# Second batch's k and q turned on TensorE instead of by the DMA crossbar, in a fused attention and FFN kernel

## The chip, the cores and the metric

The kernel runs on 1 core of one Trainium2 chip. The metric is the device time of one execution in microseconds (us), median of several runs. A run is called fast or slow; on one core a slow run is one that lies over 1.5% above the fastest of the same kernel. Profiles are of single executions; their span is about 2 us shorter than the time quoted for the same run.

Names used below: TensorE is the matmul engine (PE in the profile), VectorE is DVE, ScalarE is ACT, GpSimd is POOL, and the sync queue (SP) issues DMAs. "Turning" means transposing. SBUF and PSUM are the two on-chip memories that hold the tiles of the kernel; its matmuls write to PSUM. A "crossbar turn" is a transpose that the DMA engines do, from SBUF to SBUF. A "TensorE turn" is a matmul with an identity, followed by a copy from PSUM to SBUF on VectorE.

## The reference

Eight batches, eight heads, 576 positions, head dimension 64, feature dimension 128. All inputs and the output are float32.

```python
def phi(x):                                   # per batch and head
    proj = einsum('bhsd,df->bhsf', x, w_phi)
    proj = proj - max(abs(proj), axis=-1)
    return concatenate([exp(proj), exp(-proj)], axis=-1)
q_p, k_p = phi(q), phi(k)
kv  = einsum('bhsf,bhsd->bhfd', k_p, v)
z   = sum(k_p, axis=2)
x   = einsum('bhsf,bhfd->bhsd', q_p, kv) / (einsum('bhsf,bhf->bhs', q_p, z) + 1e-6)
x   = x.transpose(0, 2, 1, 3).reshape(4608, 512)
out = (maximum(x @ w_gate, 0) * (x @ w_val)) @ w_out      # d_ff = 1536
```

## The kernel before

The kernel lists closures at "ticks", sorts them, and emits them in that order; every engine then runs its own instructions in the emitted order. The FFN of batch g runs while the attention of batch g+1 is computed, so that TensorE always has matmuls. Batches are numbered from 0; "the second batch" is b = 1. Of the 576 positions of a batch, 512 go in four chunks of 128; the last 64 of two batches together make one shared ("mixed") chunk.

The projections need k and q with the head dimension on the partitions, so each must be turned after its load. Batch 0 is turned on TensorE, because nothing else is there to do; all later batches go through the crossbar.

```python
def turn(b, name):                                    # the crossbar
    n = H * C // 2
    t = inputs[f"{name}T", b] = sb_in.tile([P, n, P], BF16, name=f"{name}T{b % 2}")
    nc.sync.dma_start_transpose(out=t, in_=inputs[name, b].rearrange("p h c d -> p (h c d)"))

def transposed(blocks):                               # TensorE, then a VectorE copy
    n = len(blocks)
    pt = psum_a(BF16)                                 # one of five PSUM buffers "pa"
    for i, blk in enumerate(blocks):
        nc.tensor.matmul(pt[:, P * i : P * i + P], lhsT=blk, rhs=ident, is_transpose=True)
    t = sb_T.tile([P, n, P], BF16, name=f"tT{n}")
    nc.vector.tensor_copy(t.rearrange("p a b -> p (a b)"), pt[:, 0 : n * P])
    return t
# ... cut: project_rows, k_rows, k_values, k_kv, q_rows, q_cols, q_num, the FFN steps ...
    def start():                                      # k of two heads, in k_item
        if b:
            k_start(st, inputs["knT", b][:, 4 * u : 4 * u + 4], sb_k)
            return
        # ... cut: transposed() of four blocks of kn
    def turned():                                     # q of two chunks, in q_item_chunks
        if b:
            return inputs["qnT", b][:, cp :: C // 2]
        # ... cut: transposed() of eight blocks of qn
# ... cut ...
S0 = 36                                               # the FFN starts at tick 36
at(13, load_k, 1)
at(21, load_val_gate, wv_sb, moe_w_val, 1)
at(21, load_val_gate, wg_sb, moe_w_gate, 1)
at(22, load_v, 1, 0, H, nc.gpsimd)
at(33, load_val_gate, wv_sb, moe_w_val, 2)
at(33, load_val_gate, wg_sb, moe_w_gate, 2)
at(46, load_q, 1)
at(50, load_out)
at(60, load_mixed, 0, "qm", q, nc.gpsimd, BF16)
at(30, turn, 1, "kn")
at(54.5, turn, 1, "qn")
at(70, turn_mixed, 0, "qm")
```

The k items of the second batch start at ticks 40, 44, 48 and 52, its q items at 56 and 64. The loads of k, q and the weights, which cast from float32 to bfloat16, are issued from GpSimd's queue. GpSimd issues them in order with its own arithmetic.

## Time and profile before

433.88 us median of 3 runs (432.11 to 438.56).

| what | where it is read | value |
|---|---|---|
| TensorE busy, 80 to 360 us | windows | 274.3 of 280 us |
| TensorE waits for k's crossbar turn | waits of PE | 3.1 us |
| TensorE waits for q's crossbar turn | waits of PE | 11.4 us |
| k's turn, issue to landing | DMA issues | 14.1 us |
| q's turn, issue to landing | DMA issues | 13.7 us |
| granted TensorE clock, 60 to 80 us | windows | 0.69 |

The first view is the span in 40 equal slices of the kernel before; a digit is a busy share in tenths, and PEclk the granted TensorE clock in tenths.

```profile
PE   3576716998999999999999999999999999999995
PEclk9998976999999999999999999999999999999999
DMA  8999499911299239224932492249320002002004
```

TensorE is full from the eighth slice on. Time can be won before that, in the first 76 us: the fourth, sixth and seventh slices have holes, and the clock falls after the larger one.

The waits of the PE engine between 18 and 80 us (kernel before): engine, line and output, what it waited for, then us in total, times, longest.

```profile
PE pa L152 <- DMA qnT_898<-qn: 11.4, 1, 11.4
PE pa L152 <- DMA knT_496<-kn: 3.1, 1, 3.1
PE pf L252 <- ACT qp L258: 2.5, 2, 2.2
PE pa L310 <- POOL xu L303: 2.4, 3, 1.5
```

Line 152 is the projection of k or q rows: it waits for turned data. These two waits are 14.5 us of TensorE time. The chain of waits of the kernel before, cut to the DMAs and one GpSimd step (start, duration, what), tells what each turn waited for in its turn.

```profile
18.07 6.62 DMA kn<-in_k_dram
24.71 14.13 DMA knT_496<-kn
...
45.87 2.02 POOL vs L169 x2
47.88 0.07 POOL vs L175
47.96 5.98 DMA qn<-in_q_dram
53.95 13.73 DMA qnT_898<-qn
```

Both turns begin the moment their load lands, and each takes 14 us. q's load in turn is held by GpSimd's arithmetic ahead of it in the same queue. The timeline of PE (kernel before; start, duration, operation, count, idle before it) shows both waits and what comes after each.

```profile
38.89 0.61 PE L152 MATMUL pa<-w_119,knT_496 128*128 128x256 bf16 x2 [3.13 <-DMA knT_496<-kn]
39.29 1.06 PE L331 MATMUL pf<-xT,wv_sb 128*128 128x256 bf16 x4
...
67.73 0.61 PE L152 MATMUL pa<-w_119,qnT_898 128*128 128x256 bf16 x2 [11.37 <-DMA qnT_898<-qn]
68.13 1.06 PE L331 MATMUL pf<-xT,wv_sb 128*128 128x256 bf16 x4
...
86.60 1.89 PE L353 MATMUL pf<-wo_sb,h_568 128*128 128x512 bf16 x8
```

The FFN group of four 256-column matmuls takes 1.06 us after each wait; it takes 0.60 us elsewhere. The last line is the first matmul of the FFN's output, a good milestone: from it to the end of the span are 431.3 - 86.6 = 344.7 us.

### The profile page before, as it was taken

To read this page: it belongs to the slowest core of one execution; us is meant where nothing else is said; L and a number is where in the kernel's file an instruction comes from. 1 tells how busy PE (TensorE), PEld (TensorE's weight loads), DVE (VectorE), ACT (ScalarE), POOL (GpSimd) and SP (SyncE) were. 2 spreads that over 40 slices of the span, in tenths; PEclk is the share of its full clock that TensorE was granted. 3 is DMA by queue.
4 is the path that set the end of the run, shared out by engine and by line. 5 is a ranking of instruction groups with operands and counts; after the bars stand their busy time and mean duration, and the time that the engine had idled before them with its cause. 6 is when DMAs were issued, how large, how long until landed. Compare 5 with 4: busy or idle time off the path is not lost.

```text
span 431.3 us, 8204 instructions
## 1 busy us (share of the span) xinstructions
PE 387.6 (90%) x3110; PEld 219.7 (51%) x3164; DVE 262.9 (61%) x592; ACT 250.0 (58%) x575; POOL 159.0 (37%) x204
## 2 busy tenths in 40 slices
PE   3576716998999999999999999999999999999995
PEld 1455614554555555555555655555555555444442
DVE  3786513787567767875695669746966685430420
ACT  3983623654875776568667765686677652332321
POOL 8951960025541660157416601574154011000000
PEclk9998976999999999999999999999999999999999
DMA  8999499911299239224932492249320002002004
GB/s 156 192 237 143 56 178 217 161 50 49 28 181 136 81 103 186 49 75 64 222 58 76 112 207 50 74 59 218 68 74 25 2 2 98 2 0 99 0 2 97
DMA packets 78263, 41.89 MB, mean 97 GB/s; under 512 B 45776, under 2 KB 73040, under 8 KB 78224
## 3 DMA queue, kind: packets, MB, share of 16 engines
q0 software_dynamic: 30480, 16.52, 29.0%
q1 hardware_dynamic: 47744, 24.84, 24.9%
q8 instruction: 25, 0.41, 0.4%
q14 instruction: 14, 0.11, 0.1%
HBM read 37.81 MB, written 9.44 MB: 110 GB/s over the span
## 4 chain that ended last, share of the span: by engine, by line
PE 72%; DMA 11%; ACT 7%; DVE 5%; POOL 3%; issue 2%; POOLq 0%; ACTq 0%
PE pf L331 37%; PE pf L353 18%; PE pa L152 5%; PE pa L274 4%; DMA knT_496<-kn 3%; PE pa L252 3%; DMA qnT_898<-qn 3%; PE pa L228 3%; DMA kn<-in_k_dram 3%; DVE mk L157 2%; POOL vs L169 1%; DMA qn<-in_q_dram 1%; PE pa L310 1%; DVE u L298 1%; DVE t L290 1%
## 5 line engine op out<-in xcount | busy, mean ns | idle before, releaser
L331 PE MATMUL pf<-xT,wv_sb 128*128 128x512 bf16 (+1 forms) x392 | 100.1, 370 | 4.0 <-DVE xT L316 2.8
L331 PE MATMUL pf<-xT,wg_sb 128*128 128x512 bf16 (+1 forms) x391 | 98.5, 369 | 3.9 <-ACT val_sb L340 3.0
L340 ACT CAST val_sb<-pf 128x512 bf16<-128x512 f32 (+1 forms) x114 | 65.4, 574 | 62.1 <-PE pf L331 61.8
L303 POOL TENSOR_TENSOR xu<-u,r 128x512 bf16<-128x512 f32 x36 | 37.4, 1040 | 160.5 <-DVE r L301 137.3
L258 ACT ACTIVATE qp<-pa 128x512 bf16<-128x512 f32 x128 | 69.5, 604 | 12.6 <-PE pa L252 12.6
L169 POOL TENSOR_TENSOR vs<-vn,ek 128x512 bf16<-128x512 f32 x64 | 65.8, 1049 | 29.8 <-ACT ek L194 29.7
L331 PEld LDWEIGHTS <-wg_sb 128*128 128x128 bf16 x456 | 44.7, 98 | 44.4 <-issue 5.3
L331 PEld LDWEIGHTS <-wv_sb 128*128 128x128 bf16 x456 | 44.8, 99 | 42.8 <-issue 4.8
L157 DVE TENSOR_REDUCE mk<-pa 128x4 f32<-128x512 f32 x72 | 48.1, 681 | 11.2 <-PE pa L152 10.7
L274 PEld LDWEIGHTS <-qp 128*128 128x128 bf16 x640 | 34.0, 98 | 21.4 <-issue 0.9
L298 DVE TENSOR_TENSOR u<-pa,t 128x195 f32<-128x195 f32 (+3 forms) x120 | 40.4, 338 | 6.8 <-ACT t L286 0.5
L290 DVE TENSOR_TENSOR t<-pa,cq 128x195 f32<-128x195 f32 (+3 forms) x114 | 37.6, 329 | 5.7 <-PE pa L274 5.0
L363 ACT COPY out_sb<-pf 128x512 f32<-128x512 f32 x36 | 21.3, 592 | 30.3 <-PE pf L353 28.2
L274 PE MATMUL pa<-kv,qp 128*128 128x65 bf16 x640 | 37.7, 194 | 0.6 <-DVE u L298 0.5
L342 DVE SCALAR_TENSOR_TENSOR h_5920<-pf,val_sb 128x512 bf16<-128x512 f32 x12 | 8.3, 692 | 22.8 <-PE pf L331 22.8
L342 DVE SCALAR_TENSOR_TENSOR h_5699<-pf,val_sb 128x512 bf16<-128x512 f32 x12 | 8.3, 692 | 14.5 <-PE pf L331 14.5
L310 PEld LDWEIGHTS <-xu 128*128 128x128 bf16 x144 | 10.6, 98 | 11.9 <-POOL xu L303 5.3
L310 PE MATMUL pa<-ident,xu 128*128 128x128 bf16 x144 | 14.0, 219 | 2.4 <-POOL xu L303 2.4
L342 DVE SCALAR_TENSOR_TENSOR h_568<-pf,val_sb 128x256 bf16<-128x256 f32 (+1 forms) x18 | 9.1, 507 | 10.3 <-ACT val_sb L340 6.7
L342 DVE SCALAR_TENSOR_TENSOR h_1512<-pf,val_sb 128x512 bf16<-128x512 f32 x12 | 8.3, 689 | 11.4 <-ACT val_sb L340 5.2
L316 DVE COPY xT<-pa 128x512 bf16<-128x512 bf16 x32 | 13.3, 415 | 1.9 <-PE pa L310 1.7
L342 DVE SCALAR_TENSOR_TENSOR h_4371<-pf,val_sb 128x512 bf16<-128x512 f32 x12 | 8.2, 685 | 10.2 <-ACT val_sb L340 4.9
(403 smaller groups left out, 659.1 us busy)
## 6 DMA issues: line engine op xcount, KB each, us to landing
out_dram<-out_sb SPq DMA_DIRECT2D x32, 256.0 KB, 2.3
vn<-in_v_dram SPq DMA_DIRECT2D x6, 1024.0 KB, 5.9
qn<-in_q_dram POOLq DMA_DIRECT2D x8, 512.0 KB, 9.5
kn<-in_k_dram POOLq DMA_DIRECT2D x7, 512.0 KB, 6.6
wv_sb<-in_moe_w_val_dram POOLq DMA_DIRECT2D x3, 512.0 KB, 8.0
wg_sb<-in_moe_w_gate_dram POOLq DMA_DIRECT2D x3, 512.0 KB, 9.1
wo_sb<-in_moe_w_out_dram POOLq DMA_DIRECT2D x1, 1536.0 KB, 13.5
vn<-in_v_dram POOLq DMA_DIRECT2D x1, 1024.0 KB, 11.7
```

Of the source, the lines that this page charges most:

```text
L157: nc.vector.tensor_reduce(m, pp.rearrange("p (c f) -> p c f", f=F), axis=AX.X, op=ALU.max, apply_absolute_value=True,)
L169: eng.tensor_tensor(dst[:, :, s, 0:D], src, ek[:, :, s : s + 1].to_broadcast([P, 8, D]), op=ALU.mult,)
L258: nc.scalar.activation(x["qp"][:, s, slot].rearrange("p a b -> p (a b)"), pf, AF.Exp, scale=sign)
L274: nc.tensor.matmul(pn[:, E * (2 * i + s) : E * (2 * i + s + 1)], lhsT=x["qp"][:, s, slot, blk, :], rhs=kvs[b, h // 2][:, h % 2, s, :],)
L290: nc.vector.tensor_tensor(t, ab[:, :, 1], st["c"][rows, col(lo) : col(lo + n - 1) + 1 : col(1) - col(0)][:, :, None].to_broadcast([np_, n, ...
L298: nc.vector.tensor_tensor(x["u"][rows, lo : lo + n], ab[:, :, 0], t, op=ALU.add)
L303: nc.gpsimd.tensor_tensor(x["xu"], x["u"][:, :, 0:D], r.to_broadcast([P, 8, D]), op=ALU.mult)
L310: nc.tensor.matmul(pt[:, P * i : P * i + P], lhsT=x["xu"][:, 2 * i : 2 * i + 2].rearrange("p a d -> p (a d)"), rhs=ident, is_transpose=True,)
L331: nc.tensor.matmul(ps, lhsT=w[:, dc, P * fi : P * fi + P], rhs=xT[:, dc, lo:hi], start=(dc == 0), stop=(dc == NDC - 1),)
L340: nc.scalar.copy(st["val"], ps)
L342: nc.vector.scalar_tensor_tensor(st["h2"][:, fi, lo:hi], ps, 0.0, st["val"], op0=ALU.max, op1=ALU.mult)
L353: nc.tensor.matmul(st["po"], lhsT=st["h2"][:, fi, P * t : P * t + P], rhs=wo_sb[:, fi, :], start=(fi == 0), stop=(fi == NFC - 1),)
```

## The change

Batch 1's k and q are no longer given to the crossbar, and the two closures ask whether a turned tile exists instead of asking whether b is above 0. The load of a later batch's q moves by half a tick, so that it is emitted after the second q turn of the batch before it, which now reads the same buffer on TensorE at tick t + 24. The intent is to take the crossbar's latency off the start-up.

```diff
@@ k_item
-            if b:
+            if ("knT", b) in inputs:
                 k_start(st, inputs["knT", b][:, 4 * u : 4 * u + 4], sb_k)
                 return
@@ q_item_chunks
-            if b:
+            if ("qnT", b) in inputs:
                 return inputs["qnT", b][:, cp :: C // 2]
@@ start-up schedule
-    at(30, turn, 1, "kn")
-    at(54.5, turn, 1, "qn")
     at(70, turn_mixed, 0, "qm")
@@ loop over batches
-            at(t + 24, load_q, b + 1)
+            at(t + 24.5, load_q, b + 1)
```

## The prediction

> **What bounds the kernel now.** From about 76 us on TensorE does: 98 to 99% busy in the windows from 76 to 360 us. Before that it waits. The waits of the PE engine between 18 and 80 us name two crossbar turns: 11.4 us on qnT_898 (56.4 to 67.7 us) and 3.1 us on knT_496 (35.8 to 38.9 us). The chain of waits holds both: knT_496 from 24.7 us for 14.1 us, qnT_898 from 54.0 us for 13.7 us. Each begins as its load lands. Both run beside loads; later turns of the same size take 4.3 to 12.1 us. That agrees with the Trainium skill, "DMA: Bandwidth & Descriptors", section "Issuing engines are not separate DMA queues": DMAs from all queues interleave on the same 16 engines.
>
> The waits also chill the clock: 0.69 mean granted in 60 to 80 us. After each wait a group of four 256-column FFN matmuls takes 1.06 us, elsewhere 0.60 us. The skill's "TensorE: Matmul & The Clock Gate", Part 1, says that an idle window of about 3.4 us halves the clock; the trace agrees. I estimate 1.4 us and 2 us lost this way.
>
> **Removed.** Two turns (512 KB each), both waits, most cold stretches: at most 3.1 + 1.4 + 11.4 + 2 = 18 us.
>
> **Added.** 32 turns on TensorE: eight took 0.61 us including latency, so about 0.06 us each, 1.8 us, partly in gaps. Six copies on VectorE: 4 x 0.42 and 2 x 0.69 = 3.1 us.
>
> **How much is on the path.** At the first wait not all 4.5 us come back: VectorE is busy until 37.5 us, and its first k reduction (39.5 us) can only move to about 38.0 us with a copy ahead of it. I expect ekm, GpSimd's work and the load of batch 1's q (issued at 48.0 us, 6.0 us to landing) to move about 2 us: qn lands near 52 us. TensorE reaches its q turns, two FFN half steps before the old wait, at about 52 us too: at most 1 us of the 11.4 us stays. q rows then start near 55.2 us instead of 67.7; with 2 us of cold clock gone and 0.5 us of turns added, the kernel is about 14 us ahead at the old 76 us mark.
>
> Downstream TensorE bounds it, and batch 2's data had slack. qmT landed at 79.2 us and was first used at 88.5; kmT 83.3 and 93.7; knT_1184 82.8 and 99.0. Their loads start 2 to 9 us sooner and the DMA engines lose 1 MB of turns, so I expect them 5 to 9 us earlier; qmT and kmT keep some 3 us of slack.
>
> **Prediction.** 420 us, 8 in 10 between 416 and 425. Faster by over 2%: 0.91; within 2%: 0.08; slower: 0.01.
>
> **What would show it.** PE's waits name neither turn of batch 1; PE idle before its q turns under 1 us. Granted clock of 0.95 or more in 40 to 80 us. First wo_sb matmul near 73 us instead of 86.6; from there to the end about as long as before (345 us). VectorE busy +3.1 us, PE +1.5 to 3 us.
>
> **What would make it wrong.** Less gain: VectorE, near 75% busy from 36 to 56 us with the copies, holds rows and PSUM; qn lands late; qmT or kmT, needed 14 us sooner, become the new wait. More gain: other waits in 40 to 56 us came from the cold start.

## The result, and the profile after

417.79 us median (417.4 to 418.31, 4 runs, all fast), against 433.85 us for the kernel before (4 runs). The ratio of fast runs is 0.9614, with a 95% interval from 0.9538 to 0.969: faster. Ratios here are the mean time of one kernel's fast runs over that of the other's in the same rounds, so not quite the ratio of the medians that are quoted.

The span in slices, kernel after:

```profile
PE   3677899989999999999999999999999999999995
PEclk9999999999999999999999999999999999999999
DMA  7996699812994393149812971379210002002004
```

The holes are gone and the clock never falls. The waits of PE between 18 and 80 us, kernel after:

```profile
PE pf L252 <- ACT qp L258: 1.9, 2, 1.6
PE pa L310 <- POOL xu L303: 1.6, 3, 0.7
PE pa L152 <- DVE tT_719 L145: 1.1, 1, 1.1
...
PE pa L152 <- DMA qmT<-qm: 0.6, 1, 0.6
```

Neither turn of batch 1 is there. Two new small waits are: 1.1 us for the VectorE copy of the second k turn (tT_719), which stands in VectorE's queue behind work for batch 0; and 0.6 us for the crossbar turn of the mixed q chunk, which is now wanted 15 us sooner. The timeline of PE, kernel after:

```profile
35.77 0.39 PE L152 MATMUL pa<-w_119,tT_618 128*128 128x256 bf16 x2
35.99 0.60 PE L331 MATMUL pf<-xT,wv_sb 128*128 128x256 bf16 x4
...
51.25 0.62 PE L141 MATMUL pa<-ident,qn 128*128 128x128 bf16 x8
51.71 0.60 PE L331 MATMUL pf<-xT,wv_sb 128*128 128x256 bf16 x4
...
53.70 0.39 PE L152 MATMUL pa<-w_119,tT_949 128*128 128x256 bf16 x2
...
70.70 1.89 PE L353 MATMUL pf<-wo_sb,h_566 128*128 128x512 bf16 x8
```

The k rows start at 35.8 instead of 38.9 us, the q rows at 53.7 instead of 67.7 us, the FFN's output at 70.7 instead of 86.6 us. The four-matmul group takes 0.60 us after both places. The milestones give the account of the profiled runs:

| stretch | before | after | gained |
|---|---|---|---|
| start to load of batch 1's q issued | 47.96 | 45.45 | 2.5 us |
| from there to the first q rows | 19.8 | 8.2 | 11.5 us |
| q rows to first output matmul | 18.9 | 17.0 | 1.9 us |
| first output matmul to end of span | 344.7 | 345.5 | -0.8 us |
| span | 431.3 | 416.2 | 15.1 us |

One caution on such comparisons: even before anything differs, traces are not level. The load of batch 1's k is issued at 18.07 us in the kernel before, at 17.71 us in the changed kernel, and anywhere up to 19.07 us in the runs below. So 0.36 of the first row's 2.5 us is this offset, and 2.15 us are gained after it.

### The profile page after: what moved, and what is told of

The parts are those of the page before. It is cut to its first block, busy times and chain, and to the rows that moved or that the text cites. A ratio compares the mean times of both kernels' runs of the same rounds, so it can differ in the third digit from the quotient of the medians.

```text
span 416.2 us, 8326 instructions
## 1 busy us (share of the span) xinstructions
PE 389.9 (94%) x3196; PEld 219.9 (53%) x3196; DVE 265.6 (64%) x598; ACT 250.0 (60%) x575; POOL 159.1 (38%) x204
## 4 chain that ended last, share of the span: by engine, by line
PE 70%; ACT 9%; DVE 9%; DMA 6%; POOL 3%; issue 2%; DVEq 0%; ACTq 0%; SPq 0%; POOLq 0%
PE pf L331 35%; PE pf L353 18%; PE pa L152 5%; PE pa L228 4%; PE pa L274 3%; PE pa L252 3%; DMA qm<-in_q_dram 2%; DMA qn<-in_q_dram 2%; DVE mk L157 2%; DVE u L298 2%; DVE t L290 2%; DMA qmT<-qm 1%; PE pa L310 1%; ACT val_sb L340 1%; ACT qp L258 1%
## 5 line engine op out<-in xcount | busy, mean ns | idle before, releaser
L331 PE MATMUL pf<-xT,wg_sb 128*128 128x512 bf16 (+1 forms) x408 | 99.6, 367 | 2.5 <-ACT val_sb L340 2.5
L303 POOL TENSOR_TENSOR xu<-u,r 128x512 bf16<-128x512 f32 x36 | 37.4, 1040 | 152.5 <-DVE r L301 133.5
L310 PEld LDWEIGHTS <-xu 128*128 128x128 bf16 x144 | 10.5, 98 | 11.9 <-POOL xu L303 4.5
L342 DVE SCALAR_TENSOR_TENSOR h_1558<-pf,val_sb 128x512 bf16<-128x512 f32 x12 | 8.3, 689 | 11.4 <-ACT val_sb L340 5.2
L342 DVE SCALAR_TENSOR_TENSOR h_4417<-pf,val_sb 128x512 bf16<-128x512 f32 x12 | 8.2, 685 | 10.2 <-ACT val_sb L340 4.9
```

What stands on the lines that cost most here:

```text
L303: nc.gpsimd.tensor_tensor(x["xu"], x["u"][:, :, 0:D], r.to_broadcast([P, 8, D]), op=ALU.mult)
L310: nc.tensor.matmul(pt[:, P * i : P * i + P], lhsT=x["xu"][:, 2 * i : 2 * i + 2].rearrange("p a d -> p (a d)"), rhs=ident, is_transpose=True,)
L331: nc.tensor.matmul(ps, lhsT=w[:, dc, P * fi : P * fi + P], rhs=xT[:, dc, lo:hi], start=(dc == 0), stop=(dc == NDC - 1),)
L342: nc.vector.scalar_tensor_tensor(st["h2"][:, fi, lo:hi], ps, 0.0, st["val"], op0=ALU.max, op1=ALU.mult)
```

## The experiments

All gave correct results. e1 to e4, e5 to e8 and e9 to e12 each shared a chip and the runs of the kernel before; "before" varies from group to group, so the ratio or the trace decides, not a difference of medians across groups.

| label | what it is | median (range), us | ratio to before, 95% |
|---|---|---|---|
| e1_q_only | only q on TensorE | 421.3 (417.5 to 424.4) | 0.964, 0.953 to 0.975 |
| e2_k_only | only k on TensorE | 432.3 (431.8 to 433.5) | 0.9925, 0.984 to 1.001 |
| e3_spare_turns | both on TensorE, crossbar turns done for nobody | 426.3 (425.3 to 427.2) | 0.978, 0.970 to 0.986 |
| e4_all_tensor | all batches on TensorE | 428.2 (426.8 to 429.3) | 0.982, 0.972 to 0.992 |
| e5_warm_wait | before, with matmuls in the wait | 433.3 (431.4 to 441.6) | 0.990, 0.981 to 1.000 |
| e6_q_load_early | q by the crossbar, loaded earlier | 418.7 (417.7 to 419.7) | 0.959, 0.954 to 0.965 |
| e7_and_qm_early | the same, mixed q earlier too | 418.2 (417.1 to 419.3) | 0.958, 0.953 to 0.963 |
| e8_after_qm_early | changed kernel, mixed q earlier | 418.4 (418.1 to 419.7) | 0.959, 0.954 to 0.964 |
| e9_after_again | changed kernel, unedited | 418.8 (418.0 to 419.6) | 0.963, 0.958 to 0.968 |
| e10_spare_shared_early | e3, shared chunks early | 420.8 (420.1 to 422.3) | 0.968, 0.963 to 0.974 |
| e11_before_slice_late | before, last weight slices later | 436.1 (435.7 to 437.2) | 1.003, 0.999 to 1.008 |
| e12_crossbar_reordered | both by the crossbar, loads reordered | 422.4 (420.4 to 426.9) | 0.970, 0.965 to 0.975 |

The theory (T): the gain is the latency that the crossbar turns put between a landed load and its first reader on TensorE. The rivals: R1, the gain is DMA traffic taken away (1 MB of turns); R2, only q counts, since k's wait was hidden behind q's; R3 and R4, crossbar turns are slow wherever they stand.

### One half of the change alone: e1_q_only and e2_k_only

```diff
 # e1: the changed kernel, plus
+    at(30, turn, 1, "kn")
 # e2: the changed kernel, plus
+    at(54.5, turn, 1, "qn")
```

> Only q of the second batch on TensorE, its k by the crossbar again. Theory T (the gain is the time that the two crossbar turns added between a landed load and its first reader, each on its own): the wait of 3 us on knT before the first k rows comes back, with a cold clock after it; the wait on q does not. About 2.5 us slower than the changed kernel: 420 to 421.5 us. Rival R1 (the gain is DMA traffic taken away, half of it each): about 426 us. Rival R2 (k was hidden behind the wait on q, so only q counts): 418 us.

> Only k on TensorE, q by the crossbar again. Theory T: q's load is issued about 2.5 us sooner than in the kernel before (45.5 instead of 48.0 us), then the crossbar turn takes its 13 us again with TensorE idle for about 11 us: 430.5 to 432 us. R1: about 426 us. R2: 434 us, as before.

Measured: 421.3 and 432.3 us. The first waits of PE in each (18 to 90 us), e1_q_only and then e2_k_only:

```profile
PE pa L152 <- DMA knT<-kn: 3.6, 1, 3.6
```

```profile
PE pa L152 <- DMA qnT<-qn: 11.9, 1, 11.9
```

Each undone half brings its own wait back. q's half makes nearly the whole gain. R1, with half of the gain for each, falls on both. R2 is refuted by e1's trace, whose FFN output starts at 74.2 us instead of 70.7 (2.6 us later if both are counted from the issue of batch 1's k load), but the times are less sharp: e1's runs spread over 7 us, from 417.5 (as fast as the changed kernel) to 424.4 us (a slow run). k's half alone has no clear gain: its interval includes 1. That is a little less than expected (430.5 to 432). Its trace tells one reason: the profiled run had a clock of 0.80 granted between 20 and 26 us, where the changed kernel had 1.00. Batch 0's matmuls of k with v that stand there (line 228) take 5.2 us instead of 3.1, and q's load was issued at 47.85 us. Of these 2.4 us behind the changed kernel, 0.9 were there before 20 us (k's load at 18.60 us), and the rest fits the slow stretch. The Trainium skill, "TensorE: Matmul & The Clock Gate", Part 1, says that the window which decides the clock runs freely, so that the number of slow matmuls differs between runs of one kernel. These two traces, of two kernels that are the same up to there, fit that; that it is the reason is not shown. e2 also holds the half-tick move of the later q loads, so that move by itself has no clear gain either.

### The crossbar turns done for nobody: e3_spare_turns and e10_spare_shared_early

```diff
 # e3: the changed kernel, plus
+    def turn_spare(b, name):                 # as turn(), but nobody reads the tile
+        t = sb_in.tile([P, H * C // 2, P], BF16, name=f"{name}T{b % 2}")
+        nc.sync.dma_start_transpose(out=t, in_=inputs[name, b].rearrange("p h c d -> p (h c d)"))
+    at(30, turn_spare, 1, "kn")
+    at(54.5, turn_spare, 1, "qn")
 # e10: e3, and
-    at(60, load_mixed, 0, "qm", q, nc.gpsimd, BF16)
-    at(70, turn_mixed, 0, "qm")
+    at(34.5, load_mixed, 0, "qm", q, nc.gpsimd, BF16)
+    at(34.6, load_mixed, 1, "km", k, nc.gpsimd, BF16)    # later mixed chunks as before
+    at(41, turn_mixed, 0, "qm")
+    at(41.5, turn_mixed, 1, "km")
```

> Both on TensorE as in the changed kernel, and both crossbar turns of the kernel before done as well, into tiles that nobody reads. The DMA engines move the bytes of the kernel before; TensorE waits for none of them. Theory T: 418 to 421 us, what is lost coming from the sync queue, whose issue of the spare q turn delays batch 2's v and the turn of the mixed q. R1 (DMA traffic is the cause): near 430 us.

> The run with the spare crossbar turns lost 5 us and more, and its trace shows a wait of 4.6 us on qmT. Here the spare turns stay, but the shared chunks (mixed q and k) are loaded and turned early, at ticks 34.5 and 41, ahead of the spare q turn on the sync queue. If the loss came through the late shared chunks alone (theory T): within 2 us of the changed kernel, no wait on qmT or kmT. If the bytes of the spare turns themselves slow the start-up (R1): again 5 us or more slower than the changed kernel.

e3 took 426.3 us: neither the 418 to 421 of T nor the 430 of R1. My expectation was too low, and the trace names the term. e3_spare_turns, its largest wait of PE, then its sync queue:

```profile
PE pa L156 <- DMA qmT<-qm: 4.6, 1, 4.6
```

```profile
53.26 7.96 SPq L114 DMA_TRANSPOSE qnT<-qn  x1
61.40 1.48 SPq L92 DMA_DIRECT2D vm<-in_v_dram  x2
63.00 2.15 SPq L84 DMA_DIRECT2D vn<-in_v_dram  x1
69.73 1.78 SPq L118 DMA_TRANSPOSE qmT<-qm  x1
```

The spare q turn holds the sync queue for 8 us. Batch 2's v is then issued at 63.0 us instead of 55.8 us in the changed kernel. The mixed q's turn follows at 69.7 instead of 67.4 us, and lands 9.2 us later instead of 6.0. TensorE stands 4.6 us before it, and its clock falls again.

e10 keeps the spare turns and takes the mixed chunks out of their way: 420.8 us, 2.1 us above the changed kernel of the same rounds (418.8). What is left has a name too; e10_spare_shared_early, GpSimd's timeline and then PE's:

```profile
72.36 0.89 POOL L84 DMA_DIRECT2D qn<-in_q_dram  x1 [14.11 <-PE pf L335]
73.27 2.05 POOL L307 TENSOR_TENSOR xu<-u,r 128x512 bf16<-128x512 f32 x2
```

```profile
74.38 0.40 PE L314 MATMUL pa<-ident,xu 128*128 128x128 bf16 x4 [2.13 <-POOL xu L307]
```

GpSimd's queue stood 14.1 us before the load of batch 2's q. (That load overwrites the buffer that the spare turn reads. The timeline names another releaser, but the chain of waits leads from this load back to the spare q turn, which runs from 53.35 us for 17.95 us.) The arithmetic behind it came late, and TensorE waited 2.1 us. So in the form that R1 had, that bytes on the DMA engines slow the start-up by themselves, it is not supported: with the same turns in flight, the ratio to the kernel before is 0.968 where the changed kernel has 0.963. The spare k turn of e10 even took 19.9 us to land, and nothing waited for it. But a part of the prize, some 7 us in e3 (0.978 against 0.963), hangs on the queues that a long turn blocks, which the prediction did not price.

### TensorE turns for every batch: e4_all_tensor

```diff
-            at(t + 24.5, load_q, b + 1)
-            at(t + 30, turn, b + 1, "kn")
-            at(t + 34, turn, b + 1, "qn")
+            at(t + 28.5, load_q, b + 1)          # after the last TensorE reader
```

> k and q of every batch on TensorE, no crossbar turn but those of the mixed chunks. Theory T: from the third batch on the crossbar's latency is hidden and TensorE is 99 % busy, so six batches x 32 turns x 0.056 us add 10 to 11 us: 427 to 430 us, with TensorE busy 10 us longer and still no waits. Rival R3 (a crossbar turn costs time wherever it stands, TensorE turns fit in gaps): at or below 418 us.

428.2 us, as T said. First line of part 1 of the profile's page, e4_all_tensor and then the changed kernel:

```profile
PE 401.1 (94%) x3388; PEld 232.0 (54%) x3388; DVE 281.6 (66%) x634; ACT 250.4 (59%) x575; POOL 159.7 (37%) x204
```

```profile
PE 389.9 (94%) x3196; PEld 219.9 (53%) x3196; DVE 265.6 (64%) x598; ACT 250.0 (60%) x575; POOL 159.1 (38%) x204
```

192 more turns make TensorE busy 11.2 us longer, and from the first output matmul (72.9 us) to the end pass 353.9 us instead of 345.5. In the steady part TensorE has no room, and the crossbar's latency there is hidden, so the crossbar is the right place there. The change pays only at the start-up.

### The cold clock: e5_warm_wait

```diff
 # the kernel before, plus
+    def filler(n):
+        pa = psum_a()
+        for i in range(n):
+            nc.tensor.matmul(pa, lhsT=wv_sb[:, i % NDC, 0:P], rhs=wg_sb[:, i % NDC, 0:512])
+    at(57.9, filler, 48)
```

> The kernel before, with 48 matmuls of 512 columns (about 10.4 us, results read by nobody) ahead of the q rows of batch 1, in the wait for the crossbar turn. The wait keeps its length but TensorE does not idle. If the cold clock after the wait cost 2 us as predicted: 2 us faster than before, about 432 us, four 256-column matmuls after the wait take 0.60 us and the clock stays at 1.0 from 67 to 72 us. If the cold clock is hidden behind other engines: no difference, 434 us.

The times alone are weak: 431.4 to 433.3 us in the four fast runs, ratio 0.990 with an interval that reaches 1.000. The trace is clearer. e5_warm_wait, PE:

```profile
63.62 10.52 PE L115 MATMUL pa<-wg_sb,wv_sb 128*128 128x512 bf16 x48
...
76.71 0.39 PE L157 MATMUL pa<-w,qnT 128*128 128x256 bf16 x2 [1.96 <-DMA qnT<-qn]
76.94 0.60 PE L336 MATMUL pf<-xT,wv_sb 128*128 128x256 bf16 x4
...
93.26 1.89 PE L358 MATMUL pf<-wo_sb,h 128*128 128x512 bf16 x8
```

From the q rows to the first output matmul pass 93.26 - 76.71 = 16.55 us, against 18.87 in the kernel before: same instructions, crossbar-turned q in both. So the cold clock after q's wait cost 2.3 us. This does not hang on e5 alone, whose profiled run was a slow one: the stretch is 16.55 us as well in e6, e7 and e12, fast runs whose q comes from the crossbar with no wait before it. With the wait, it is 18.08 us in e2 and 19.19 in e11, so the cost there was 1.5 and 2.6 us. The changed kernel takes 17.00 us there, since it does the second group of q turns in this stretch; 0.45 us is what these cost.

In e5's profiled run everything is later: its k turn was waited for 10.2 us, not 3.1. This turned out to be a lead (see e11).

### The crossbar with an earlier load: e6, e7, e8

```diff
 # e6: the changed kernel, but
-    at(46, load_q, 1)
+    at(34, load_q, 1)
+    at(40, turn, 1, "qn")
 # e7: e6, and e8: the changed kernel, with
-    at(60, load_mixed, 0, "qm", q, nc.gpsimd, BF16)
-    at(70, turn_mixed, 0, "qm")
+    at(34.5, load_mixed, 0, "qm", q, nc.gpsimd, BF16)
+    at(41, turn_mixed, 0, "qm")
```

> The changed kernel, but q of batch 1 turned by the crossbar again, with its load issued at tick 34 (about 32 us) instead of tick 46. Theory T says that the crossbar did harm only since its turn began when TensorE was nearly there: here the turn should be done by about 47 us, before the q rows at 53.7 us, so no wait on it: as fast as the changed kernel or faster by up to 1 us, since TensorE and VectorE are spared 16 turns and 2 copies: 416.5 to 418 us. Rival R4 (the crossbar beside loads is too slow in the start-up whatever the order): over 424 us.

> As the last, and the mixed q chunk loaded at tick 34.5 and turned at tick 41 instead of 60 and 70. The 0.6 us wait of TensorE on qmT should go: 0.5 to 1 us faster than the last one, 416 to 417.5 us. If that wait was covered by VectorE's lag: no difference.

> The changed kernel with the mixed q chunk alone loaded and turned earlier (tick 34.5 and 41). The wait of 0.6 us on qmT goes: 417 to 417.5 us. If nothing else moves, this is what the last term of the prediction (slack of the shared chunks) cost.

e6 is level with the changed kernel, with q through the crossbar. Its sync queue, then PE:

```profile
43.32 2.02 SPq L110 DMA_TRANSPOSE qnT<-qn  x1
```

```profile
54.98 0.38 PE L152 MATMUL pa<-w,qnT 128*128 128x256 bf16 x2
...
71.53 1.89 PE L353 MATMUL pf<-wo_sb,h 128*128 128x512 bf16 x8
```

The turn was issued at 43.3 us and landed 4.4 us later, and TensorE did not wait for it. This settles the theory for q: neither the crossbar nor TensorE is the point, but whether the turned data are there when TensorE comes by. The hoped-for extra 0.5 to 1 us of e7 and e8 is not there: both traces have lost the wait on qmT, but the times, 418.2 and 418.4 us, cannot be told from 418.8 for the changed kernel (e9) or from e6. In the traces, the stretch from the first output matmul to the end is 344.7 us in e8 against 345.5 in the changed kernel, a gain that the times do not resolve.

### Why the kernel before spreads: e9, e11 and e12

```diff
 # e11: the kernel before, but (e12: e7 with k's crossbar turn back, and)
-    at(33, load_val_gate, wv_sb, moe_w_val, 2)
-    at(33, load_val_gate, wg_sb, moe_w_gate, 2)
+    at(44.5, load_val_gate, wv_sb, moe_w_val, 2)
+    at(44.5, load_val_gate, wg_sb, moe_w_gate, 2)
```

> The changed kernel itself, unedited, as the reference for the other three runs on the same chip. 417 to 419 us, with a spread under 2 us, while the kernel before spreads over 431 to 440 us as in the earlier rounds.

> The kernel before with one edit: the last slices of the two FFN weights are loaded at tick 44.5 instead of 33, after the crossbar turn of k. The traces of before and of a slow run show the DMA engines at about 50 GB/s in stretches while that turn and casting loads are in flight together (7 us late in the slow run). Theory: k's turn lands by 35 us, the wait of 3.1 us goes, and with it the spread: 429 to 432 us in all runs. Rival: the spread of the kernel before comes from elsewhere (clock, chip state): 433 us and up to 440 us as before.

> Neither k nor q of the second batch on TensorE: both by the crossbar as in the kernel before, but q's and the mixed q chunk's loads issued at tick 34, the last weight slices at tick 44.5. Theory T (latency in the wrong place, not the crossbar as such): neither turn is waited for; as fast as the changed kernel or 1 to 2 us faster (no turns on TensorE, no copies on VectorE): 415.5 to 418 us. If a crossbar turn in the start-up costs time whatever the order: over 424 us.

The kernel before ran from 432.1 to 442.7 us in these rounds, 11 runs, two of them slow; the changed kernel from 418.0 to 419.6. The waits of PE, e11_before_slice_late and e12_crossbar_reordered:

```profile
PE pa L152 <- DMA qnT<-qn: 13.4, 1, 13.4
...
PE pa L152 <- DMA knT<-kn: 0.6, 1, 0.6
```

```profile
PE pa L152 <- DMA knT<-kn: 3.4, 1, 3.4
```

In e11, k's turn lands 11.9 us after its issue instead of 14.1, its wait falls from 3.1 to 0.6 us, and the spread is gone: 435.7 to 437.2 us in six runs. But it is not faster, against my expectation: the two slices now run beside q's load, which takes 7.5 us instead of 6.0. They have landed before q's turn begins, but w_out's load, queued behind them, lands 15.5 us after its issue instead of 13.5; q's turn beside it takes 15.05 us instead of 13.73, and q's wait grows by 2 us. What was taken from one wait was given to the next.

In e12, q's load took the place of the slices beside k's turn, which then took 15.1 us; TensorE waited 3.4 us for it, and the runs spread again, from 420.4 to 426.9 us. q's own turn landed in 4.4 us, unwaited. So e12 missed its 415.5 to 418 us by what k's turn costs in that place. For q a reordering does as well as TensorE; for k, whose load lands at 24.7 us and which is wanted at 35.8 us amid the weight loads, I found none that does.

The spread goes with one thing in all the kernels run. Where the trace shows TensorE waiting for a k turn of 14 us or more, runs range over 6.4 us or more (before, e1, e5, e12). In all others, each kernel taken in its own rounds, they range over 2.5 us or less. With fast runs alone this holds for the kernel before (5.6 to 6.5 us in each group) and weakly for e1 (3.8 us); e5 and e12 then range over 1.9 and 2.2 us, so their spread is that of three slow runs of seven and one of six. The one slow run with a trace, e5's, shows such a wait grown to 10.2 us. Its window from 34 to 43.5 us, cut to the queues:

```profile
q1 hardware_dynamic: 1385, 0.35, 91.0%
q0 software_dynamic: 211, 0.24, 48.6%
...
knT<-kn SPq DMA_TRANSPOSE x1, 20.1
```

(Packets, MB, share of 16 engines; the last line is the turn, issued earlier, and its time to landing.) The DMA engines are fully taken, mostly by the turn, yet moved 0.6 MB in 9.5 us, 63 GB/s. The kernel before has such a stretch too, but a short one: 55 GB/s from 35.5 to 37.5 us. Over the whole k turn it moved 198 GB/s, and e5 152 GB/s. A turn of 19.9 us stands in a fast run as well (e10), where TensorE does not wait for it. Why turns and loads slow each other down, and why by so much in some runs, these runs do not show. That the other slow runs were slow for the same reason is likely, not shown, since they have no trace.

## Why the prediction was right

The forecast was 420 us, 416 to 425; measured were 417.8. Point by point:

- **What bounds the kernel, and what is removed.** Right. Both waits went, and with them the cold clock; the clock is 1.00 in the windows from 40 to 60 and from 60 to 80 us (forecast: 0.95 or more).
- **The first wait gives back about 2 us, not 4.5.** Right: q's load moved from 47.96 to 45.45 us, 2.5 us, of which 2.15 us are gained after k's load. The reason given, that VectorE holds k's chain, shows as the 1.1 us wait for tT_719. The named reduction moved from 39.5 to 37.4 us, a little more than the 38.0 expected.
- **At most 1 us of the 11.4 us stays.** Right, and none stayed: the load lands as TensorE arrives at 51.25 us. That is close: TensorE waited 0.9 and 0.7 us for the same load in e3 and e10. q rows were forecast at 55.2 us and came at 53.7, or 1.1 us early when both are counted from k's load; that is about half of the 2 us by which the forecast was too slow. The term mis-sized is this one. Another 1 us is in no trace: the two profiled spans differ by 15.1 us, the medians by 16.1.
- **2 us of cold clock, 0.5 us of turns.** Measured: 2.3 us (e5 against before) and 0.45 us (changed kernel against e5). What lowers the clock is less simple than the idle window that the prediction names: in e3 and e10 it fell to 0.50 after a wait of 1.1 us for VectorE at 42 us, and the same wait left it at 1.00 in the changed kernel.
- **The lead is kept to the end.** Nearly: 0.8 us are given back after the first output matmul, 0.6 of it in the wait on qmT that the prediction had named as a danger. The slack of some 3 us that it left to qmT and kmT is the term that failed: both landed about 6 us earlier, within the forecast 5 to 9, but were wanted 15 us earlier, so that qmT came 0.6 us late (73.4 us) and kmT had 1.3 us left. e8 shows that taking it away does not visibly change the time.
- **Busy times.** VectorE rose by 2.7 us (forecast 3.1), TensorE by 2.3 (1.5 to 3); the latter is loose, since the trace of before lacks 54 matmul records against its weight loads.

What the prediction did not have: that k's turn, only 3.1 us of wait in the one trace at hand, goes with how much the time varies (the spread left with it in e2 and e11, and stayed in e1); and that a long turn also blocks the queue it is issued from (e3).

## What to carry to other kernels

A transfer is cheap or dear by when its result is wanted: the same crossbar turn cost 11.4 us on q at the start, nothing on q when loaded some 15 us sooner (33.3 instead of 48.0 us), and saved 8 us against TensorE turns in the steady part. So price a move between engines stage by stage, and try an earlier load first. And before trusting the size of a wait on a contended DMA from one trace, look at the spread of the runs.

## What the Trainium skill lacked or had wrong

- "DMA: Bandwidth & Descriptors", section "DMA Transpose (X-bar)": it has no time for a turn beside other loads. A turn of 512 KB took 4.4 us from issue to landing when the engines had little else (e6). Beside the start-up's loads it took 11.9 to 15.7 us, 17.9 and 19.9 us in e10, and 20.1 us in e5's slow run.
- The same page, section "Latency and other measured facts", gives 261 GB/s for a transpose whose middle dimension is not contiguous, more for a contiguous one. The best turn here, 4.2 us for 512 KB from issue to landing (a later turn of e6), is 125 GB/s. The page does not say whether its figure counts all of that time, so the two may measure different things.
- "TensorE: Matmul & The Clock Gate", Part 4, gives about 275 ns for a 128x128 turn in one kernel's context, and says that the full clock does not engage for turns. It has no figure for turns in a stream of matmuls. Here one turn lasted 0.22 us, somewhat less than the page's figure, and eight of them moved TensorE on by 0.45 us in all, 56 ns each (8 turns of q at 60.4 us in the changed kernel), at a granted clock of 1.00. Whether turns alone would raise the clock, no run shows.
- No page gives the time for which a turn holds its issuing queue beside other loads: the sync queue was busy 6.3 to 8.4 us with one turn of 512 KB beside the start-up's loads, and 2.0 us with one issued when the engines had little else (e6).
